# Seven block products for the last two tiles of the first layer, second-layer weights begun during the later attention pairs, k tail on 128 rows

## The chip, the cores and the metric

The kernel runs on one core of one Trainium2 chip. The metric is the device time of one execution in microseconds: before the change the median of three runs is 967.34 us (967.02 to 968.44).

## The reference, cut to what matters

Three parts, one behind the other, all in float32 (the weights of the two layers arrive as float64):

```python
def phi(x):                                   # attention features, 64 -> 2 x 128
    proj = x @ w_phi
    proj = proj - max(abs(proj), axis=-1)
    return concat([exp(proj), exp(-proj)])
num = phi(q) @ (phi(k).T @ v)                 # for 4 batches x 8 heads, 576 positions, 64 wide
den = phi(q) @ sum(phi(k)) + 1e-06
x = reshape(num / den)                        # 2304 x 512
h = x @ w_in;   x = maximum(0.01 * h, h) @ w_out      # first layer, 512 -> 2048 -> 512
h = x @ w_in2;  out = (h * sigmoid(h)) @ w_out2       # second layer, 512 -> 2048 -> 512
```

## The kernel before, in words

**Number format.** TensorE multiplies in the fast rounded form of float32. To keep the precision every operand is split into a rounded high part and the rest (`split`, L428: ScalarE copies into the rounded form, VectorE subtracts through `sub`, L125), and each product is three matmuls: high by high, high by low, low by high.

**Attention.** Heads are taken in 16 pairs. Pairs 0 to 7 are "full" pairs: plain float32 matmuls, which the machine does in two passes. Pairs 8 to 15 are "split" pairs with the three-matmul form; their denominators take a round trip through DRAM (`num_split`, L323: `e<-d`, `rec<-e`, `d<-rec`). The last 64 positions of k, the k tail, are done by `s_pkt` (L190): for a full pair by a matmul with 64 contraction rows (`kt[0:64]` by `wraw[0:64]`). The array `kt` already holds the tail twice, in rows 0 to 63 and 64 to 127; `BDF[:, 0]` is w_phi in rows 0 to 63 and zeros in rows 64 to 127. GpSimd finds the largest magnitude of each column over the partitions (`partition_all_reduce`, L227).

**Layer 1.** The 2304 rows of x are five tiles (`tiles1`, L86): two of 462 and three of 460 columns, as x is held transposed. For each tile t there are 16 chunks c of 128 of the 2048 hidden features. A step (t, c) is `emit_h` (L526: 12 matmuls, the leaky ReLU on ScalarE, the split into `gh` and `gl`) and, one step later, `emit_y` (L542: 12 matmuls into the four `y` banks of PSUM, which all 16 chunks of a tile fill). So a tile has 192 matmuls of each kind. In tile 0 the output weights are converted from float64 and saved in `wos`; later tiles load them again (`load_wo`, L488).

**Weights of layer 2.** Layer 2 works by seven block products in place of eight (the list `PRODUCTS`, L522). Its weights are made in 16 jobs (`prep_w7`, L446): two float64 loads with conversions (`load64`, `narrow64`), four sums, four splits and stores to `w7s`. `run_jobs` (L741) spends a credit per step; a job costs 1.8 + 1.8 + 1.8 + 1.6 = 7.0 credits. Before the change it starts when the last attention step has been issued, with 3.4 credits a step. The loads use three rotating buffers (`raw`).

**Order.** The program order of attention against layer 1 comes from due times: attention steps have offsets (`OFF0`, `OFF1`), layer-1 steps have a time `T0 + pace(s + 1)` for s = 16 t + c (L712 to L716), and `run_att` issues what is due. From that program a planner makes each engine's fixed queue when the kernel is built: it plays the program through with assumed durations and lets each engine take the ready instruction that stands first in the program. So work far down in the program can be placed early if its inputs and buffers are there. On the chip each queue is strictly in order. All loads and stores but two go through one queue, SP's. The first twelve weight loads are held back by tokens: GpSimd copies one number, which exists only after a given pair's `partition_all_reduce`, into the buffer that the load then overwrites (`PACE`, L68; L406 to L409).

## Time and profile before

| | before |
|---|---|
| median of the runs | 967.34 us |
| profiled execution | 967.73 us, span 965.9 us, mean granted clock 0.998 |
| TensorE (PE) busy | 947.5 us, 98% of the span |
| weight loads (PEld) busy | 886.1 us, 92% |
| VectorE (DVE) busy | 648.7 us, 67% |
| ScalarE (ACT) busy | 597.1 us, 62% |
| GpSimd (POOL) busy | 78.4 us, 8% |
| HBM read, written | 177.82 MB, 47.22 MB |

Busy times are a union over an engine's instructions. Matmuls overlap in the array, so the duration of one (some 370 ns in layer 1) is not its cost; its cost is the distance to the next one's start. The shares are averages over the span, and the stages differ, so the rows below are by stretch.

Attention's full pairs run from the start to about 110 us; the first matmul of layer 1 starts at 113.7 us, and the split pairs run between layer 1's matmuls until about 410 us. Layer 1 alone, with the weight jobs, runs to 613 us, layer 2 from there to the end (its first products start earlier, between the last steps of layer 1).

### The profile page before, as it was taken

The numbers are of one execution on the slowest core, as the hardware profiler recorded it, in microseconds if no ns is written. First come the engines' busy times: TensorE is split into PE (matmuls) and PEld (weight loads), VectorE is DVE, ScalarE is ACT, GpSimd is POOL, SyncE is SP. The second block draws the span as 40 slices with busy tenths as digits, with TensorE's granted clock in tenths as the row PEclk, the third lists the DMA queues.
The fourth block names the chain that finished last, engine by engine and source line by source line (L and its number), as shares of the span: only waits on it lengthen the run. The fifth ranks groups of instructions, "written<-read, shape, count | busy, mean of one in ns | idle before, by whom it ended". The sixth has DMA issues, their size and how long they took to land.

```text
span 965.9 us, 15759 instructions
## 1 busy us (share of the span) xinstructions
PE 947.5 (98%) x5376; PEld 886.1 (92%) x5376; DVE 648.7 (67%) x1279; ACT 597.1 (62%) x1224; POOL 78.4 (8%) x56
## 2 busy tenths in 40 slices
PE   7999999989999999999999999999999999999998
PEld 6888888979899999988888999999999999999998
DVE  6677799985666665278777767778762585624853
ACT  6567687867777777466656556556554565544553
POOL 3334300121111101000000000000000000000000
PEclk9999999999999999999999999999999999999999
DMA  6333477873344232299999999896989778997884
GB/s 218 100 108 102 154 242 252 304 245 118 96 118 119 93 106 93 90 321 367 377 345 318 373 356 353 281 371 233 320 285 297 239 234 271 291 294 216 249 278 138
DMA packets 102384, 226.13 MB, mean 234 GB/s; under 512 B 15008, under 2 KB 24992, under 8 KB 102304
## 3 DMA queue, kind: packets, MB, share of 16 engines
q1 hardware_dynamic: 102016, 224.86, 69.5%
q8 instruction: 43, 0.70, 0.3%
q14 instruction: 37, 0.30, 0.1%
q10 hardware_dynamic: 288, 0.26, 0.1%
HBM read 177.82 MB, written 47.22 MB: 233 GB/s over the span
## 4 chain that ended last, share of the span: by engine, by line
PE 80%; DMA 8%; DVE 6%; ACT 4%; issue 1%; SPq 1%; DVEq 0%; ACTq 0%
PE ps_y L688 18%; PE ps_y L552 17%; PE ps_a L533 16%; PE ps_a L612 10%; PE ps_y L612 8%; PE ps_a L268 2%; PE ps_a L302 2%; DMA d<-rec 2%; PE ps_a L334 2%; DMA rec<-e 1%; PE ps_y L268 1%; DMA e<-d 1%; DMA raw<-in_moe_w_in_dram 1%; PE ps_a L180 1%; DMA w7s<-wst 1%
## 5 line engine op out<-in xcount | busy, mean ns | idle before, releaser
L552 PE MATMUL ps_y<-gh,wo 128*128 128x460 f32 (+1 forms) x640 | 198.6, 374 | 1.9 <-ACT gh L429 1.9
L688 PE MATMUL ps_y<-gt,ws 128*128 128x384 f32 x1008 | 177.2, 336 | 0.0
L688 PEld LDWEIGHTS ps_y<-gt,ws 128*128 128x128 f32 x1008 | 176.5, 188 | 0.0
L552 PEld LDWEIGHTS ps_y<-gh,wo 128*128 128x128 f32 x640 | 120.5, 189 | 16.2 <-ACT gh L429 3.1
L552 PE MATMUL ps_y<-gl,wo 128*128 128x460 f32 (+1 forms) x320 | 118.3, 374 | 3.0 <-DVE gl L126 3.0
L533 PE MATMUL ps_a<-xh,wih 128*128 128x460 f32 (+1 forms) x320 | 119.5, 373 | 0.3 <-ACT g L536 0.3
L533 PE MATMUL ps_a<-xl,wih 128*128 128x460 f32 (+1 forms) x320 | 118.8, 371 | 0.0
L533 PE MATMUL ps_a<-xh,wil 128*128 128x460 f32 (+1 forms) x320 | 118.7, 371 | 0.0
L612 PE MATMUL ps_a<-xs,ws 128*128 128x384 f32 x546 | 105.0, 338 | 0.5 <-DMA ws<-w7s 0.5
L612 PEld LDWEIGHTS ps_a<-xs,ws 128*128 128x128 f32 x546 | 96.8, 188 | 1.3 <-ACT g L604 0.8
L227 POOL PARTITION_ALL_REDUCE m<-p x32 | 72.8, 2279 | 297.3 <-ACT p L223 199.5
L429 ACT ACTIVATE gt<-g 128x384 fp32r<-128x384 f32 x120 | 62.8, 524 | 51.9 <-PE ps_y L688 49.8
L126 DVE TENSOR_TENSOR gt<-g,gt 128x384 fp32r<-128x384 f32 x120 | 66.5, 556 | 33.1 <-ACT gt L429 32.6
L612 PE MATMUL ps_y<-xs,ws 128*128 128x384 f32 x462 | 88.3, 338 | 0.2 <-DVE g L588 0.2
L612 PEld LDWEIGHTS ps_y<-xs,ws 128*128 128x128 f32 x462 | 81.7, 188 | 0.6 <-DVE g L588 0.5
L126 DVE TENSOR_TENSOR gl<-g,gh 128x460 fp32r<-128x460 f32 (+1 forms) x80 | 51.7, 647 | 33.4 <-ACT gh L429 30.4
L552 PEld LDWEIGHTS ps_y<-gl,wo 128*128 128x128 f32 x320 | 60.6, 190 | 10.6 <-DVE gl L126 3.9
L533 PEld LDWEIGHTS ps_a<-xh,wil 128*128 128x128 f32 x320 | 60.1, 188 | 6.8
L533 PEld LDWEIGHTS ps_a<-xh,wih 128*128 128x128 f32 x320 | 60.2, 188 | 6.7 <-ACT g L536 0.5
L533 PEld LDWEIGHTS ps_a<-xl,wih 128*128 128x128 f32 x320 | 60.2, 188 | 5.9
L536 ACT ACTIVATE g<-ps_a 128x460 f32<-128x460 f32 (+1 forms) x80 | 44.0, 552 | 34.6 <-PE ps_a L533 32.8
L420 ACT ACTIVATE t<-raw 128x512 f32<-128x512 f32 x64 | 42.6, 668 | 15.1 <-DVE wst L126 6.5
(142 smaller groups left out, 1560.2 us busy)
## 6 DMA issues: line engine op xcount, KB each, us to landing
ws<-w7s SPq DMA_DIRECT2D x336, 256.0 KB, 3.8
wo<-wos SPq DMA_DIRECT2D x64, 512.0 KB, 5.4
w7s<-wst SPq DMA_DIRECT2D x48, 512.0 KB, 5.9
raw<-in_moe_w_in_dram SPq DMA_DIRECT2D x32, 512.0 KB, 5.0
raw<-in_moe_w_out_dram SPq DMA_DIRECT2D x32, 512.0 KB, 5.8
wos<-wo SPq DMA_DIRECT2D x16, 512.0 KB, 3.1
va<-in_v_dram SPq DMA_DIRECT2D x16, 325.0 KB, 3.6
qr<-in_q_dram SPq DMA_DIRECT2D x16, 288.0 KB, 3.8
```

The lines of the kernel that those rows point to most:

```text
L126: nc.vector.tensor_tensor(out_, x, h.bitcast(F32), op=ALU.subtract)
L227: nc.gpsimd.partition_all_reduce(m, p, 128, bass_isa.ReduceOp.absmax)
L268: nc.tensor.matmul(pv[:, s, j], ke[:, 2 * c + j, s, :], vf[:, w : w + NKV], start=False, stop=(j == 1 and c == 3), skip_group_check=True)
L302: nc.tensor.matmul(pb[:, w : w + NNUM], e[:, s, cs], KV[:, s, j], start=(s == 0), stop=(s == 1))
L334: nc.tensor.matmul(o, lhs, st[m, a][:, s, j * w : (j + 1) * w], start=(n == 0), stop=(n == 5))
L420: nc.scalar.activation(t, hi.bitcast(F32), AF.Abs)
L429: nc.scalar.activation(h, f, AF.Copy)
L533: nc.tensor.matmul(ph, a[:, kk, :], b_[:, kk, :], start=(m == 0), stop=(m == 3 * KD - 1))
L536: nc.scalar.activation(g, ph, AF.Prelu, alpha=0.01)
L552: nc.tensor.matmul(Y[t][d][:, 0:n], a[:, ds_], b_, start=(c == 0 and m == 0), stop=(c == NC - 1 and m == 2))
L612: nc.tensor.matmul(bank[b_], w[:, a, kk], x[:, c, kk], start=(first and m == 0), stop=(m == 5), skip_group_check=True)
L688: nc.tensor.matmul(bank[b_][db], w[:, a, db], t[:, c], start=(first and p == 0 and m == 0), stop=(p == NP - 1 and m == 2), skip_group_chec ...
```

## The change

Four edits, in one diff:

1. Tiles 3 and 4 (`TA`, `TB`) are taken together for x W_in: two tiles by two chunks make a 2 x 2 block product over two halves of the 512 contraction rows, done by the seven products of `PRODUCTS`, each of six matmuls (`h1_ops`). The sums of x are made once (`prep_x1`), those of the weights for every pair of chunks (`combine`). Results of tile TA are split and used at once; those of TB are kept in float32 in `G4` (in buffers of the weights no longer needed) and split later (`split_g4`), and TB's output products come last, on their own.
2. The layer-2 weight jobs begin at step s = 17 with 2.0 credits a step while attention is still running; then 3.4 a step, 4.0 a pair of chunks, 1.0 a chunk of TB. Loads issued while attention is unfinished wait for a token of the last `partition_all_reduce` that was issued. In that stage the stores' buffers are taken from `raw` too.
3. The k tail of a full pair is a matmul on all 128 rows.
4. Buffers are moved between pools (`attc`, `w2`, `s0`), so that the new tiles fit.

```diff
-    WH = const.tile([128, F], F32R, name="WH")
+    WH = attc.tile([128, F], F32R, name="WH")
...
-            nc.tensor.matmul(o, st["kt"][0:64], wraw[0:64], start=True, stop=True)
+            nc.tensor.matmul(o, st["kt"], BDF[:, 0], start=True, stop=True)
...
-            if a == 1 and full(i):
+            if not full(i):
+                last[0] = 2 * i + a
+                nc.gpsimd.tensor_copy(token[:, last[0] : last[0] + 1], m[0:1, 0:1])
+            elif a == 1:
...
-        if nconv[0] < len(PACE) and PACE[nconv[0]] is not None:
-
+        if nconv[0] < len(PACE):
             g = PACE[nconv[0]]
+        else:
+            g = last[0] if nconv[0] >= 2 * NC and seq else None
+        if g is not None:
             nc.gpsimd.tensor_copy(raw.bitcast(F32)[0:1, 0, 0:1], token[:, g : g + 1])
...
-            o = wp.tile([128, m, 2, 256], F32R, tag="wo1", bufs=WOB, name="wst")
+            if w2p[0] is None:
+                o = wp.tile([128, m, 2, 256], F32R, tag="raw", bufs=RAWB, name="wst")
+            else:
+                o = wp.tile([128, m, 2, 256], F32R, tag="wo1", bufs=WOB, name="wst")
...
+    def prep_x1():
+
+        for i in (2, 3, 4, 5):
+            TX[i] = s0p[0].tile([128, 2, 2, N1], F32R, tag="tx", bufs=4, name="tx")
+        for kk in range(2):
+            b = []
+            for k_ in (kk, kk + 2):
+                b1 = wp.tile([128, 2, N1], F32, tag="raw", bufs=RAWB, name="b1")
+                for j, t in enumerate((TA, TB)):
+                    xh, xl = X1[t]
+                    nc.vector.tensor_tensor(b1[:, j], xh[:, k_].bitcast(F32), xl[:, k_].bitcast(F32), op=ALU.add)
+                b.append(b1)
+            b1, b2 = b
...
+            nc.vector.tensor_tensor(t1, b1[:, 1], b1[:, 0], op=ALU.subtract)
+            nc.vector.tensor_tensor(t2, b2[:, 1], t1, op=ALU.subtract)
+            nc.vector.tensor_tensor(t3, b2[:, 1], b1[:, 1], op=ALU.subtract)
+            nc.vector.tensor_tensor(t4, b2[:, 0], t2, op=ALU.subtract)
+            for i, x in ((4, t2), (5, t3), (3, t1), (2, t4)):
+                split(x, TX[i][:, 0, kk], TX[i][:, 1, kk])
+
+    def combine(p):
+
+        f = []
+        for c in (2 * p, 2 * p + 1):
+            x = s0p[0].tile([128, 512], F32, tag=f"f{c % 2}", name="f")
+            h, l = (w.rearrange("p k f -> p (k f)").bitcast(F32) for w in wi[0, c])
+            nc.vector.tensor_tensor(x, h, l, op=ALU.add)
+            f.append(x)
+        fa, fb = f
+        lo, hi = slice(0, 256), slice(256, 512)
+        nc.vector.tensor_tensor(fb[:, hi], fb[:, lo], fb[:, hi], op=ALU.add)
+        nc.vector.tensor_tensor(fb[:, lo], fa[:, lo], fb[:, lo], op=ALU.subtract)
+        nc.vector.tensor_tensor(fa[:, lo], fb[:, hi], fa[:, lo], op=ALU.subtract)
+        nc.vector.tensor_tensor(fa[:, hi], fa[:, hi], fa[:, lo], op=ALU.subtract)
+        for x, ids in ((fa, (4, 6)), (fb, (5, 3))):
+            o = s0p[0].tile([128, 2, 2, 2, 128], F32R, tag="cw", bufs=4, name="cw")
+            split(x, o[:, 0].rearrange("p m k f -> p (m k f)"), o[:, 1].rearrange("p m k f -> p (m k f)"))
...
+    def h1_ops(p):
+
+        bank = [ps("a")[:, 0:N1], ps("a")[:, 0:N1]]
...
+        for n, (b_, wi_, xi, first) in enumerate(PRODUCTS):
+            m = 0
+            for kk in range(2):
+                for a, c in ((0, 0), (0, 1), (1, 0)):
+                    nc.tensor.matmul(bank[b_], w1_of(p, wi_, a, kk), x1_of(xi, c, kk), start=(first and m == 0), stop=(m == 5), skip_group_check=True)
+                    m += 1
+            if n == 0:
+                v1 = hold(bank[0])
+            elif n == 1:
+                leaky(2 * p, 0, bank[1], v1)
+            elif n == 2:
+                u2 = hold(bank[0])
+            elif n == 3:
+                v7 = hold(bank[1])
+            elif n == 4:
+                leaky(2 * p + 1, 1, bank[0], v7)
+            elif n == 5:
+                leaky(2 * p + 1, 0, bank[1], u2)
+            else:
+                leaky(2 * p, 1, bank[0])
+            yield
...
-    RATE = (3.4, 9.0)
+    RATE = (2.0, 3.4, 4.0, 1.0, 9.0)
...
+    def close_att():
+        att_ctx.close()
+        w2p[0] = ctx.enter_context(tc.tile_pool(name="w2", bufs=1))
+        s0p[0] = s0_ctx.enter_context(tc.tile_pool(name="s0", bufs=1))
+        settle()
+        prep_x1()
+        combine(0)
+
+    for s, (t, c) in enumerate((t, c) for t in range(TA) for c in range(NC)):
...
-        if not seq and s1p[0] is None:
-            att_ctx.close()
-            s1p[0] = ctx.enter_context(tc.tile_pool(name="s1", bufs=1))
-        if s1p[0] is not None:
-            run_jobs(RATE[0])
...
+        if s > NC:
+            run_jobs(RATE[w2p[0] is not None])
+        if not seq and w2p[0] is None:
+            close_att()
...
+    ys = y_groups(*prev)
+    for p in range(NC // 2):
+        for c in (2 * p, 2 * p + 1):
+            wo[c] = load_wo(c)
+        if p + 1 < NC // 2:
+            combine(p + 1)
+        for _ in h1_ops(p):
+            next(ys, None)
+        for _ in ys:
+            pass
+        ys = (y for c in (2 * p, 2 * p + 1) for y in y_groups(TA, c))
+        run_jobs(RATE[2])
...
+    for c in range(NC):
+        if c + 3 < NC:
+            wo[c + 3] = load_wo(c + 3)
+            split_g4(c + 3)
+        emit_y(TB, c)
+        run_jobs(RATE[3])
+        if c in (1, 4):
+            settle()
+            next(x_first)
+        if c >= 9:
+            next(h_first)
```

In `h1_ops`, `hold(x)` is a ScalarE copy out of the bank, and `leaky(c, j, x, v)` adds the held value on VectorE (where there is one), applies the leaky ReLU on ScalarE and, for TA (j = 0), splits. `y_groups` is `emit_y` given out in groups of three matmuls, one for each of the four `y` banks.

## Rows read from the trace of the kernel before

**Rows 1.** The page: engine PE's busy time; shares of the chain that ended last.

```profile
PE 947.5 (98%) x5376; PEld 886.1 (92%) x5376; DVE 648.7 (67%) x1279; ACT 597.1 (62%) x1224; POOL 78.4 (8%) x56
...
PE 80%; DMA 8%; DVE 6%; ACT 4%; issue 1%; SPq 1%; DVEq 0%; ACTq 0%
```

**Rows 2.** Windows: stretch, length; busy us (instructions) per engine; clock, DMA share, GB/s.

```profile
125.00:200.00 75.00, 71.69 (x362) 63.84 (x360) 71.32 (x136) 58.56 (x109) 5.24 (x2) 1.00 0.79 268
200.00:225.00 25.00, 25.00 (x147) 23.33 (x148) 19.30 (x38) 19.00 (x41) 3.28 (x2) 0.93 0.66 218
225.00:400.00 175.00, 174.09 (x1062) 162.14 (x1061) 99.92 (x197) 123.63 (x270) 27.19 (x13) 1.00 0.35 102
400.00:425.00 25.00, 23.41 (x112) 20.35 (x111) 12.79 (x27) 11.61 (x24) 0.00 (x0) 1.00 0.67 227
425.00:550.00 125.00, 125.00 (x600) 112.40 (x599) 98.04 (x193) 75.41 (x140) 0.00 (x0) 1.00 0.98 353
...
615.00:950.00 335.00, 334.35 (x1902) 333.46 (x1901) 207.84 (x403) 182.24 (x381) 0.00 (x0) 1.00 0.85 276
```

**Rows 3.** Timeline of PE around one k tail: start, duration, instruction, count.

```profile
32.83 0.61 PE L302 MATMUL ps_a<-KV,qh 128*128 128x96 f32 x4
33.37 0.48 PE L195 MATMUL ps_a<-wc,kt 64*128 64x128 f32 x2
33.79 0.70 PE L180 MATMUL ps_a<-wc,kr 128*128 128x256 f32 x2
```

**Rows 4.** Timeline of PE, 195 to 208 us (idle before it, releaser, in brackets).

```profile
195.89 1.10 PE L552 MATMUL ps_y<-gh,wo 128*128 128x462 f32 x4 [0.33 <-ACT gh L429]
199.97 0.47 PE L552 MATMUL ps_y<-gl,wo 128*128 128x462 f32 x1 [2.98 <-DVE gl L126]
...
206.05 1.93 PE L268 MATMUL ps_a<-va,ke 128*128 128x112 f32 x16
207.82 0.40 PE L262 MATMUL ps_a<-va,ke 128*128 128x130 f32 x2
```

**Rows 5.** Timeline of DVE in the same stretch.

```profile
197.05 1.52 DVE L422 TENSOR_SCALAR t<-t 128x512 f32<-128x512 f32 x1
...
199.29 0.63 DVE L126 TENSOR_TENSOR gl<-g,gh 128x462 fp32r<-128x462 f32 x1
```

**Rows 6.** Timeline of POOL in the same stretch.

```profile
196.62 2.69 POOL L227 PARTITION_ALL_REDUCE m<-p  x1 [13.42 <-DVE ql L126]
```

**Rows 7.** Timeline of SP's queue: loads of layer-2 weights before 225 us.

```profile
183.73 0.33 SPq L411 DMA_DIRECT2D raw<-in_moe_w_in_dram  x1
...
207.93 0.49 SPq L411 DMA_DIRECT2D raw<-in_moe_w_in_dram  x1
```

**Rows 8.** Groups by line, whole span: count; busy us, mean ns; idle before, releasers.

```profile
L126 DVE TENSOR_TENSOR gl<-g,gh 128x460 fp32r<-128x460 f32 (+1 forms) x80 | 51.7, 647 | 33.4 <-ACT gh L429 30.4 <-PE ps_y L552 2.6
L429 ACT ACTIVATE gh<-g 128x460 fp32r<-128x460 f32 (+1 forms) x80 | 46.8, 584 | 6.8 <-PE ps_y L552 5.6
L424 DVE SCALAR_TENSOR_TENSOR t<-raw,t 128x512 uint32<-128x512 uint32 x64 | 45.8, 718 | 0.9
...
L420 ACT ACTIVATE t<-raw 128x512 f32<-128x512 f32 x64 | 42.6, 668 | 15.1 <-DVE wst L126 6.5 <-DVE r L425 3.7 <-DMA raw<-in_moe_w_in_dram 2.6
...
L422 DVE TENSOR_SCALAR t<-t 128x512 f32<-128x512 f32 x64 | 29.5, 462 | 13.2 <-ACT t L420 12.2
...
L126 DVE TENSOR_TENSOR wst<-s,wst 128x512 fp32r<-128x512 f32 x32 | 22.0, 689 | 10.9 <-ACT wst L429 10.8
...
L588 DVE TENSOR_TENSOR g<-ps_a,hs 128x384 f32<-128x384 f32 x39 | 21.7, 557 | 29.2 <-PE ps_a L612 29.0
...
L356 DVE TENSOR_TENSOR x<-x,d 128x288 f32<-128x288 f32 x16 | 7.3, 459 | 33.1 <-DMA d<-rec 33.1
...
L466 DVE TENSOR_TENSOR s<-r,s 128x256 f32<-128x256 f32 x16 | 6.8, 423 | 0.4
```

**Rows 9.** DMA issues in 425 to 550 us: count, KB each, median us to landing.

```profile
wo<-wos SPq DMA_DIRECT2D x25, 512.0 KB, 6.2
```

More of the change, by code (lines that the diff above doesn't have):

```diff
@@ L104, in tile_linear_attention_ffn_ffn @@
     P = [dict() for _ in range(B * HP)]
-    token = const.tile([1, NFULL], F32, name="token")
+    token = const.tile([1, 2 * B * HP], F32, name="token")
+    last = [None]
     nconv = [0]
@@ L547, in emit_y, with group @@
             Y[t] = [ps("y") for _ in range(KD)]
-        for d in range(KD):
+        def group(d):
             ds_ = slice(d * 128, (d + 1) * 128)
+            y = Y[t][d][:, 0:n]
             for m in range(3):
                 a, b_ = ((oh, gh), (oh, gl), (ol, gh))[m]
-                nc.tensor.matmul(Y[t][d][:, 0:n], a[:, ds_], b_, start=(c == 0 and m == 0), stop=(c == NC - 1 and m == 2))
-        if c == NC - 1:
-            for d, y in enumerate(Y.pop(t)):
+                nc.tensor.matmul(y, a[:, ds_], b_, start=(c == 0 and m == 0), stop=(c == NC - 1 and m == 2))
+            if c == NC - 1:
@@ L555, in emit_y @@
                 o = gp.tile([128, n], F32, tag="o", name="o", bufs=3)
                 if d % 2 == 0:
-                    nc.vector.tensor_copy(o, y[:, 0:n])
+                    nc.vector.tensor_copy(o, y)
                 else:
-                    nc.scalar.activation(o, y[:, 0:n], AF.Copy)
+                    nc.scalar.activation(o, y, AF.Copy)
                 nc.sync.dma_start(x2[d, :, tiles1[t][0] : tiles1[t][0] + n], o)
+        for d in range(KD):
+            yield group(d)
+    def emit_y(t, c):
+        for _ in y_groups(t, c):
+            pass
@@ new lines, in tile_linear_attention_ffn_ffn @@
+    TA, TB = len(tiles1) - 2, len(tiles1) - 1
+    N1 = tiles1[TA][1]
+    TX, CW = {}, {}
+    def prep_x1():
[10 more added lines that the diff above has]
+            b1, b2 = b
+            t1, t3 = (wp.tile([128, N1], F32, tag="t64", bufs=2, name="t1") for _ in range(2))
+            t2, t4 = (wp.tile([128, N1], F32, tag="r64", bufs=2, name="t2") for _ in range(2))
+            nc.vector.tensor_tensor(t1, b1[:, 1], b1[:, 0], op=ALU.subtract)
[4 more added lines that the diff above has]
+                split(x, TX[i][:, 0, kk], TX[i][:, 1, kk])
@@ new lines, in w1_of, with x1_of, hold, leaky @@
+    def w1_of(p, i, a, kk):
+        if i < 3:
+            return wi[0, 2 * p + (i == 2)][a][:, kk + 2 * (i > 0), :]
+        return CW[p, i][:, a, kk]
+    def x1_of(i, a, kk):
+        if i in TX:
+            return TX[i][:, a, kk]
+        return X1[TB if i == 6 else TA][a][:, kk + 2 * (i > 0), :]
+    def h1_ops(p):
+        bank = [ps("a")[:, 0:N1], ps("a")[:, 0:N1]]
+        def hold(x):
+            v = gp.tile([128, N1], F32, tag="o", name="o", bufs=3)
+            nc.scalar.activation(v, x, AF.Copy)
+            return v
+        def leaky(c, j, x, v=None):
+            if j:
+                g = wp.tile([128, N1], F32, tag="wil", bufs=NC, name="g4")
+            else:
+                g = gp.tile([128, N1], F32, tag="g", name="g", bufs=2)
+            if v is not None:
+                nc.vector.tensor_tensor(g, x, v, op=ALU.add)
+                x = g
+            nc.scalar.activation(g, x, AF.Prelu, alpha=0.01)
+            if j:
+                G4[c] = g
+                return
+            gh = gp.tile([128, N1], F32R, tag="gh", name="gh", bufs=2)
+            gl = gp.tile([128, N1], F32R, tag="gl", name="gl", bufs=2)
+            split(g, gh, gl)
+            G[TA, c] = (gh, gl)
+        for n, (b_, wi_, xi, first) in enumerate(PRODUCTS):
[16 more added lines that the diff above has]
+                leaky(2 * p + 1, 0, bank[1], u2)
+            else:
+                leaky(2 * p, 1, bank[0])
+            yield
@@ L562, in tile_linear_attention_ffn_ffn, with split_g4 @@
+    G4 = {}
+    def split_g4(c):
+        tags = ("g", "g") if c % 3 == 2 else ("gh", "gl")
+        gh, gl = (gp.tile([128, N1], F32R, tag=tag, name="gh", bufs=2) for tag in tags)
+        split(G4.pop(c), gh, gl)
+        G[TB, c] = (gh, gl)
     WS = {}
@@ L657, in operand @@
             else:
[L658 removed]
+                t = w2p[0].tile([128, 2, NB], F32R, tag="wo2", bufs=4, name="gt")
             tl.append(t)
@@ L757, in tile_linear_attention_ffn_ffn @@
         prev = (t, c)
-        if not seq and s1p[0] is None:
-            att_ctx.close()
-            s1p[0] = ctx.enter_context(tc.tile_pool(name="s1", bufs=1))
-        if s1p[0] is not None:
-            run_jobs(RATE[0])
-            if t == len(tiles1) - 1:
-                if c in (2, 5):
-                    settle()
-                    next(x_first)
-                if c >= 9:
-                    next(h_first)
-    emit_y(*prev)
+        if s > NC:
+            run_jobs(RATE[w2p[0] is not None])
+        if not seq and w2p[0] is None:
+            close_att()
+    run_att(1e9)
+    if w2p[0] is None:
+        close_att()
+    ys = y_groups(*prev)
[7 more added lines that the diff above has]
+        for _ in ys:
+            pass
+        ys = (y for c in (2 * p, 2 * p + 1) for y in y_groups(TA, c))
+        run_jobs(RATE[2])
+    s0_ctx.close()
+    s1p[0] = ctx.enter_context(tc.tile_pool(name="s1", bufs=1))
+    for c in range(3):
+        wo[c] = load_wo(c)
+        split_g4(c)
+    for _ in ys:
+        pass
+    for c in range(NC):
[9 more added lines that the diff above has]
+            next(h_first)
     nothing = iter(())
```

20 lines of the change are left out of this document (11 added, 9 removed).

## Prediction

> **What bounds the kernel now.** I read the page first: PE is busy for 947.5 of 965.9 us, and the chain that ended last lies on PE for 80% of the span [rows 1]. An average over stages can hide a stage with another limit, so next come the windows [rows 2]. The reader is to see two things. PE has no idle time that matters from 225 to 400 us (174.09 of 175), from 425 to 550 us (125.00 of 125) and in layer 2 (334.35 of 335). It loses time in two places: 3.3 us in 125 to 200 us, with the granted clock at 0.93 just behind it, and 1.6 us in 400 to 425 us, where attention ends. And the other engines are not free: DVE is at 95% in 125 to 200 us (71.32 of 75), at 57% in 225 to 400, at 78% in 425 to 550; ACT at 71% in 225 to 400 and 60% in 425 to 550. So a matmul taken away is worth its full distance to the next one, as long as DVE and ACT keep up with PE; the question of this case is whether they do once the work added to them is in.
>
> **The change part by part.** The sum is made against the profiled execution, 967.73 us (span 965.9), which is 0.39 above the median of the runs, 967.34.
>
> *Products.* Tiles 3 and 4 had 2 x 16 x 12 = 384 matmuls with W_in; now 8 pairs of chunks x 7 products x 6 = 336. That is 48 fewer of 460 columns. 425 to 550 us holds only such work, 600 matmuls in 125.00 us: 0.208 us each [rows 2]. 48 x 0.208 = **-10.0 us**. The output products stay at 192 a tile.
>
> *k tail.* In a full pair the last L302 matmuls are followed by two passes with 64 rows, then by L180 [rows 3]. Sixteen float32 passes on 128 rows, 112 columns wide, take 207.82 - 206.05 = 1.77 us, 0.111 each [rows 4]. Four L302 take 0.54 us to the next start: three of 0.111, and 0.21 for the last, which has the 64-row pass behind it. The two tail passes take 0.42 to the start of L180. So 0.63 us now; with three starts 0.111 apart, 0.33. That is 0.3 us a pair, 2.4 for eight, if PE is the limit there. The trace has no 128-row tail: the bounds are -2.4 and 0 (PE only waits elsewhere). I take **-2.0**, nearer to the row, as one of eight may be hidden. [...]
>
> *Weight jobs, moved.* Five layer-2 loads were placed early by the planner, at 183.73 to 207.93 us [rows 7], and their conversions fell into the stretch where DVE is at 95%. A conversion costs DVE two operations like L422 and two like L424 (2 x 0.462 + 2 x 0.718 = 2.36 us) and ACT two like L420 (1.34) [rows 8]; five cost 11.8 and 6.7 us. In that stretch PE waits 2.98 us for `gl` [rows 4], which stands on DVE behind such work and comes at 199.29 [rows 5]; the clock dip after it costs 0.07 x 25 = 1.75 us [rows 2]. Now these loads can't be issued before s = 17, and they wait for a token. What is late next there is the last of W_out's own conversions, which stay. Bounds: -4.7 (all gone) and 0; I take **-3.0**.
>
> The jobs' new place: steps 17 to 40 (the last due attention step, 128.4, falls below T0 + pace(s + 1) first at s = 40) with 2.0 credits make 48, about seven jobs of 7.0. A job costs DVE two conversions, four sums like L466 and splits of three and a half times 0.689: 4.72 + 1.69 + 2.41 = 8.8 us; ACT four like L420 and three and a half copies like L429: 2.67 + 2.04 = 4.7 us [rows 8]. Seven jobs are 62 and 33 us. With them 225 to 400 us has DVE at 99.9 + 62 = 162 of 175 us (92%) and ACT at 123.6 + 33 = 157 (90%), in queues in strict order, where DVE already stands still for 33.1 us in all at L356, waiting for the denominators' DMAs [rows 8]. Every job also issues two loads and four stores on SP's queue, 2.8 MB, so those small DMAs wait longer. A load waits for its token on GpSimd, and behind it in that queue stands the next `partition_all_reduce`; POOL is busy for 27 of 175 us, so that has room. The nearest rows for the price in PE time are these: at DVE 78%, ACT 60% PE lost nothing in 125 us (0); at DVE 95%, ACT 78% it lost 3.3 and 1.75 us in 100 us, which over 175 us is 8.8. I take **+2.5**: PE's own work there is 98% dense, but at a lower DVE load than in the bad stretch.
>
> *End of attention.* `prep_x1` and `combine(0)` stand in the program ahead of all later steps: 24 DVE operations like `gl` (15.5 us) and 2 x 0.69 + 4 x 0.42 + 2 x 0.69 = 4.4 us, a burst of 20 us on DVE; ACT 4.7 + 1.2. All of it needs the last pair's x, so it can't be placed earlier. Behind it waits the `gl` of the following steps. PE can meanwhile do a few h blocks (12 x 0.208 = 2.5 us each, four `a` banks) and the y blocks whose `gl` is done: some 12 to 15 us. Bounds 0 and +6 (with the wait at 400 to 425 us standing as it is).
>
> *The paired tiles.* A pair of chunks is 42 + 24 = 66 matmuls, 13.7 us on PE. DVE gets `combine` 4.4, three adds like L588, wider, 0.65 each (estimate: 0.557 x 460/384), two `gl` (1.3) and 4.0/7 of a job (5.0): 12.7 us, 93%. From the burst to the end of TB DVE has some 187 us of work (nine jobs 79, `combine` 35.5, burst without it 15.5, adds 15.6, `gl` 25, x of layer 2 and the rest 16) for 185 us on PE (7 x 5.0 + 110 + 40). It fits only because jobs slip: in the window 425 to 550 us they ran behind their place in the program without PE waiting. The last jobs, of W_out2, are not needed until the output products of layer 2, where DVE is at 62%. Bounds: 0, and 5% of 150 us as in the stretch at 95%, +8. For these two parts together I take **+4.0**.
>
> *TB's output products.* A chunk is 12 x 0.208 = 2.5 us, and 512 KB of `wo` have to land in each; with loads three chunks ahead there are 7.5 us for one, against 6.2 at a DMA share of 0.98 [rows 9]. 0, as jobs are nearly out by then. The y banks change owner with no h block between, but four groups apart. If it fails, see the third rival.
>
> Pools moved, tokens copied: nothing, as POOL is free.
>
> Sum: -10.0 - 2.0 - 3.0 + 2.5 + 4.0 = -8.5, from 967.7 to 959.2; for the median 0.4 less, **958.8 us**. Its own range, with the bounds not all at one end: 953 to 965.
>
> **The rivals.**
>
> *All of the new work is hidden.* For it: in 425 to 550 us DVE at 78% cost PE nothing, and the planner can order around a burst. Against: DVE goes to over 90% for 360 us. Time: 967.3 - 10.0 - 2.4 - 4.7 = 950.2.
>
> *DVE takes PE's place, slower than before.* Place: from s = 17 to the end of TB, 175 + 185 = 360 us. Price: the lost share of the one stretch at DVE 95%, 5.05 us in 100 [rows 2], over 360 us: +18.2. Against it stand -10.0 - 2.0 - 3.0. Time: 967.3 - 15.0 + 18.2 = 970.5; a little more, 974, if ACT at 90% adds to it. It decides once PE waits for over 15 us in all. For it: 187 us of DVE work for 185 us; jobs stand ahead of `h1_ops` in program order, so PE's needs come second. Against: jobs are held back by three buffers and DMAs of 6 us, which leaves DVE gaps for the others. A collision adds to it: an L422 beside the all-reduce of 196.62 took 1.52 us [rows 5, 6] against 0.462 in the mean; 13 all-reduces in 225 to 400 us could lengthen DVE's work by 13 x 1.06 = 14 us, to 100% there. [...]
>
> *It does not do what it says: products go, time does not.* TB without h blocks has nothing to cover a late `wo`: with landings of 10 us (6.2 doubles nearly when jobs and layer 2's first loads fall into the same 40 us) a buffer comes round every 12.5 us for four chunks, 3.1 us a chunk instead of 2.5, +8 in 13 chunks; with 4.0 + 2.5 from above the sum is about 967. Against: the jobs' earlier start takes DMAs out of this time.
>
> **How the numbers follow.** Forecast 0.47, all hidden 0.20, DVE-bound 0.21, TB's loads 0.12. Faster by over 0.2% (below 965.4; 0.2% is about what a measurement of this kernel can tell): forecast, all hidden and a tenth of the last, 0.68. Within 0.2%: most of the last, 0.10. Slower: 0.22. The range goes from 949 to 974, into both sides.
>
> **What would show it.** Right: L533 down to 576 matmuls beside 336 of the new line; three starts 0.11 apart at the tail; no 3 us wait near 197 us and no dip; PE idle of no more than a few us in 225 to 400 and behind the end of attention, layer 1 ending about 8 us sooner and layer 2 unchanged. Wrong: PE waits for `gl` or a bank behind DVE, in sum over 12 us; gaps ended by `wo` in TB; DVE over 95% from the end of attention on, with the clock dipping.

## The result, and the profile after

The change makes the kernel slower: the median of four runs is 977.32 us (974.32 to 982.16), against 967.89 us for the kernel before (four runs, 967.02 to 969.47). The ratio is 1.0101, 95% interval 1.0079 to 1.0124. The forecast of 958.8 us had the wrong sign, and the time lies above its range (949 to 974). The profiled execution took 979.34 us (span 977.2), 11.3 us more span than before.

The page after, engines and the shares of the chain that ended last, against [rows 1]:

```profile
PE 942.7 (96%) x5328; PEld 876.4 (90%) x5328; DVE 697.9 (71%) x1391; ACT 618.6 (63%) x1272; POOL 90.2 (9%) x84
...
PE 65%; DMA 12%; DVE 11%; ACT 9%; issue 2%; SPq 1%; POOL 0%; DVEq 0%; ACTq 0%
```

The 48 matmuls are gone, yet PE lies on only 65% of the chain (80% before), and DMA, DVE and ACT have taken the rest. The windows say where (same columns as [rows 2]):

```profile
125.00:200.00 75.00, 72.48 (x361) 64.36 (x360) 71.37 (x136) 58.50 (x107) 7.35 (x4) 0.99 0.74 252
200.00:225.00 25.00, 24.60 (x148) 22.66 (x148) 14.53 (x27) 18.51 (x40) 5.49 (x6) 0.96 0.56 167
225.00:400.00 175.00, 162.89 (x972) 147.10 (x971) 128.04 (x253) 134.02 (x287) 33.77 (x32) 1.00 0.53 168
400.00:425.00 25.00, 23.64 (x118) 20.56 (x118) 16.82 (x37) 13.24 (x30) 1.00 (x2) 1.00 0.48 168
225.00:440.00 215.00, 198.69 (x1147) 178.38 (x1146) 156.50 (x315) 153.59 (x330) 34.77 (x34) 1.00 0.53 170
440.00:550.00 110.00, 109.13 (x515) 97.40 (x514) 101.07 (x209) 72.86 (x141) 0.00 (x0) 0.98 0.88 298
...
628.00:965.00 337.00, 336.85 (x1919) 336.36 (x1918) 202.13 (x393) 181.56 (x379) 0.00 (x0) 1.00 0.83 268
```

From 225 to 400 us PE was idle for 0.9 us before [rows 2] and is for 12.1 now. The reader is to compare two lines here. From 225 to 440 us DVE is at 73% and ACT at 71%, and PE loses 16.3 us. From 440 to 550 us DVE is at 92%, and PE loses 0.9. A busy share does not tell which stretch is the tight one; the first has attention with the denominators' round trip in it, the second hasn't.

Four marks cut the 11.3 us into stages (us from the span's start, read from PE's timeline): where the output products of step 16 begin (the first step of tile 1), where attention's last matmul ends (the start of the next one), where the output products of step 47 begin (the last step before the paired tiles), and where layer 1's output products end:

| | before | after | stage, forecast | stage, measured |
|---|---|---|---|---|
| step 16 begins | 215.9 | 213.3 | -5.0 | -2.6 |
| attention ends | 397.4 | 414.5 | +2.5 | +19.7 |
| step 47 begins | 447.7 | 467.9 | with the next | +3.1 |
| layer 1 ends | 616.6 | 628.0 | -6.0 | -8.8 |

Layer 2 takes as long as before; it carries the 11.3 us to the end.

The tail, PE's timeline of after, against [rows 3]:

```profile
32.32 1.17 PE L307 MATMUL ps_a<-KV,qh 128*128 128x96 f32 x9
33.33 0.41 PE L197 MATMUL ps_a<-wc,kt 128*128 128x128 f32 x2
33.58 0.60 PE L182 MATMUL ps_a<-wc,kr 128*128 128x256 f32 x2
```

Nine passes take 1.01 us to the first of the tail, 0.112 each, with no longer last one, and the two tail passes 0.25 to the next start instead of 0.42.

Now the pair stage. First DVE, then ACT, then PE of after, in the part where PE first loses time:

```profile
227.07 0.75 DVE L244 TENSOR_TENSOR m<-p,m 128x576 f32<-128x576 f32 x1
231.88 0.46 DVE L361 TENSOR_TENSOR x<-x,d 128x288 f32<-128x288 f32 x1 [4.06 <-DMA d<-rec]
232.26 0.75 DVE L128 TENSOR_TENSOR ql<-e,qh 128x576 fp32r<-128x576 f32 x1
...
235.30 0.43 DVE L429 TENSOR_SCALAR t<-t 128x512 f32<-128x512 f32 x1 [1.11 <-ACT t L427]
...
237.22 1.21 DVE L429 TENSOR_SCALAR t<-t 128x512 f32<-128x512 f32 x1 [0.23 <-ACT t L427]
...
239.37 0.27 DVE L128 TENSOR_TENSOR KVL<-ps_a,KVH 128x128 fp32r<-128x128 f32 x1
239.56 0.68 DVE L431 SCALAR_TENSOR_TENSOR t<-raw,t 128x512 uint32<-128x512 uint32 x1
240.16 0.68 DVE L128 TENSOR_TENSOR wst<-r,wst 128x512 fp32r<-128x512 f32 x1
240.76 0.68 DVE L432 CUSTOM_DVE_ANT_0 r<-t,r 128x1024 uint16<-128x1024 uint16 x1
241.37 0.63 DVE L128 TENSOR_TENSOR gl<-g,gh 128x462 fp32r<-128x462 f32 x1
```

```profile
228.57 0.68 ACT L256 ACTIVATE qh<-e 128x576 fp32r<-128x576 f32 x1
...
232.37 0.45 ACT L292 ACTIVATE xh<-x 128x288 fp32r<-128x288 f32 x1 [2.55 <-DVE x L361]
232.72 0.67 ACT L256 ACTIVATE qh<-m 128x576 fp32r<-128x576 f32 x1
234.61 0.66 ACT L427 ACTIVATE t<-raw 128x512 f32<-128x512 f32 x1 [1.21 <-DMA raw<-in_moe_w_in_dram]
```

```profile
238.42 0.40 PE L339 MATMUL ps_a<-qh,KVH 128*128 128x288 f32 x1 [0.36 <-ACT g L546]
239.69 0.40 PE L339 MATMUL ps_a<-qh,KVL 128*128 128x288 f32 x1 [0.75 <-DVE KVL L128]
242.05 0.48 PE L565 MATMUL ps_y<-gl,wo 128*128 128x462 f32 x1 [0.65 <-DVE gl L128]
244.72 0.40 PE L339 MATMUL ps_a<-qh,KVL 128*128 128x288 f32 x1 [0.26 <-DVE KVL L128]
246.25 0.40 PE L221 MATMUL ps_a<-qs,WH 128*128 128x288 f32 x1 [0.47 <-DVE ke L159]
247.44 0.48 PE L543 MATMUL ps_a<-xh,wih 128*128 128x462 f32 x1 [0.65 <-ACT x L343]
```

DVE stands for 4.06 us at L361, which waits for the denominators. ACT's next instruction, the split of that x, waits for L361 and stands too. DVE's queue keeps its order meanwhile: its next operation, the `ql` at 232.26 us, has had its `qh` from ACT since 229.25 us (228.57 + 0.68), and still runs only behind L361. Then comes a job: ACT waits 1.21 us for its load, DVE 1.11 us for ACT, and from 235.30 on DVE works with hardly a gap (0.23 us at 237.22), a job's operations (L429 to L432, `wst`) and what PE needs (`KVL`, `gl`) in turn. PE ran from its stock until then (one wait of 0.40 us since 205 us), and now waits for each of the latter. No single wait is long, and no single releaser stands out.

From the list of waits of 205 to 440 us (engine and line waited for: us in total, times, longest us), first before, then after:

```profile
DVE x L356 <- DMA d<-rec: 33.1, 16, 4.9
...
ACT xh L287 <- DVE x L356: 30.2, 14, 4.2
```

```profile
DVE x L361 <- DMA d<-rec: 23.2, 14, 4.1
ACT xh L292 <- DVE x L361: 19.2, 11, 3.5
...
DVE t L429 <- ACT t L427: 12.1, 9, 4.6
...
ACT t L427 <- DMA raw<-in_moe_w_in_dram: 10.7, 6, 3.5
...
PEld ps_y L565 <- DVE gl L128: 6.4, 6, 2.1
```

The wait for the denominators was there before, and longer, while PE lost 2.5 us in all in the same 235 us. The chain of waits of after from 222 to 440 us goes through it all the same:

```profile
by line: DMA d<-rec 13.6%; DMA rec<-e 13.3%; DMA e<-d 9.3%; issue 5.9%; DMA raw<-in_moe_w_in_dram 4.2%; ACT d L342 3.3%; DVE m L244 3.2%; ACT x L343 3.0%; SPq L352 2.5%; DVE wst L128 2.3%; DVE x L361 2.2%; DMA wo<-wos 2.1%; ACT ke L168 1.9%
```

The three transfers of the round trip make 36% of it, and of the thirteen lines named none is PE's. In the kernel before they make 19% of the same stretch, behind PE's own lines with 20% and 19%:

```profile
by line: PE ps_y L552 20.4%; PE ps_a L533 18.9%; DMA d<-rec 8.3%; PE ps_a L268 8.1%; PE ps_a L334 6.6%; DMA rec<-e 5.6%; DMA e<-d 4.8%; DMA w7s<-wst 3.5%; issue 1.9%; SPq L347 1.3%; DVE x L356 1.3%; PE ps_a L219 1.3%; PE ps_a L220 1.2%; PE 
```

### The profile page after: what moved, and what is told of

It is laid out like the page before. It is cut to its first block, busy times and chain, and to the rows that moved or that the text cites. A ratio compares the mean times of both kernels' runs of the same rounds, so it can differ in the third digit from the quotient of the medians.

```text
span 977.2 us, 15859 instructions
## 1 busy us (share of the span) xinstructions
PE 942.7 (96%) x5328; PEld 876.4 (90%) x5328; DVE 697.9 (71%) x1391; ACT 618.6 (63%) x1272; POOL 90.2 (9%) x84
## 4 chain that ended last, share of the span: by engine, by line
PE 65%; DMA 12%; DVE 11%; ACT 9%; issue 2%; SPq 1%; POOL 0%; DVEq 0%; ACTq 0%
PE ps_y L820 18%; PE ps_y L565 13%; PE ps_a L744 10%; PE ps_y L744 8%; PE ps_a L667 7%; PE ps_a L543 4%; DMA d<-rec 3%; DMA rec<-e 3%; DMA e<-d 2%; DMA raw<-in_moe_w_in_dram 2%; PE ps_a L307 2%; PE ps_y L273 1%; DVE m L244 1%; DVE r L432 1%; ACT d L342 1%
## 5 line engine op out<-in xcount | busy, mean ns | idle before, releaser
L565 PEld LDWEIGHTS ps_y<-gh,wo 128*128 128x128 f32 x704 | 132.9, 190 | 20.0 <-issue 3.6
L565 PE MATMUL ps_y<-gl,wo 128*128 128x462 f32 (+1 forms) x256 | 95.8, 380 | 6.7 <-DVE gl L128 6.4
L543 PE MATMUL ps_a<-xh,wih 128*128 128x462 f32 (+1 forms) x192 | 72.7, 379 | 4.5 <-DVE ke L159 1.8
L543 PE MATMUL ps_a<-xl,wih 128*128 128x462 f32 (+1 forms) x192 | 71.4, 372 | 0.0
L543 PE MATMUL ps_a<-xh,wil 128*128 128x462 f32 (+1 forms) x192 | 71.2, 371 | 0.0
L436 ACT ACTIVATE gh<-g 128x460 fp32r<-128x460 f32 (+1 forms) x80 | 46.4, 584 | 12.1 <-PE ps_y L565 10.9
L128 DVE TENSOR_TENSOR gl<-g,gh 128x462 fp32r<-128x462 f32 (+1 forms) x64 | 41.3, 647 | 13.2 <-ACT gh L436 12.6
L428 ACT ACTIVATE r<-raw 128x512 uint32<-128x512 uint32 x64 | 42.4, 668 | 8.5 <-DVE wst L128 5.2
L736 ACT ACTIVATE g<-g 128x384 f32<-128x384 f32 x72 | 37.1, 520 | 16.7 <-DVE g L720 16.5
L432 DVE CUSTOM_DVE_ANT_0 r<-t,r 128x1024 uint16<-128x1024 uint16 x64 | 45.9, 719 | 1.4
```

The source lines that it names most:

```text
L128: nc.vector.tensor_tensor(out_, x, h.bitcast(F32), op=ALU.subtract)
L428: nc.scalar.activation(r, lo, AF.Copy, scale=2.0**-29)
L432: nc.vector.tensor_tensor(r, tu, r, op=ALU.add)
L436: nc.scalar.activation(h, f, AF.Copy)
L543: nc.tensor.matmul(ph, a[:, kk, :], b_[:, kk, :], start=(m == 0), stop=(m == 3 * KD - 1))
L565: nc.tensor.matmul(y, a[:, ds_], b_, start=(c == 0 and m == 0), stop=(c == NC - 1 and m == 2))
```

## The experiments

The theory at this point: the jobs' place is the whole loss, and it is lost not to a full engine but to queues in strict order, which stand at the denominators' round trip; the jobs take the slack that hid it. The rivals: DVE has no room (the forecast's second rival), the jobs' DMAs delay the small ones, and the end of attention with the paired tiles is too dense.

**Is it the moved jobs?** One kernel leaves them until attention is over, one has them alone, one takes their token away.

```diff
-    RATE = (2.0, 3.4, 4.0, 1.0, 9.0)          # e1, from after
+    RATE = (0.0, 3.4, 4.0, 1.0, 9.0)
...
+        if s > NC and s1p[0] is None:          # e2, from before; with the tokens of after
+            run_jobs(2.0)
...
-            g = last[0] if nconv[0] >= 2 * NC and seq else None      # e3, from after
+            g = None
```

> The changed kernel with RATE[0] = 0: no weight job is issued before attention ends; all 16 then follow at the later rates. If the moved jobs are the whole loss (they cost some 20 us between 205 and 440 us), PE is dense there again (attention's last output matmul near 397 us, as before, less 2) and the time falls from 977 to 955-962, unless the backlog of 16 jobs now makes DVE the limit in the paired tiles: then PE shows waits for DVE between 460 and 620 us and the time is 962-972. If the loss has another cause (the pools moved, the planner's order as a whole), the stretch 205 to 440 us stays 20 us too long and the time stays above 970.

> The kernel before plus only the moved jobs (2.0 credits a step from s = 17, tokens, stores from the raw buffers). If the move alone makes the loss: 985-992, PE waits of some 20 us between 205 and 440 us. If the loss needs the products or the tail edit beside it: 965-970.

> The changed kernel without the token in the moved loads, so that they are issued as soon as a buffer is free and land before they are needed. If ACT's waits for late loads and GpSimd's waits for raw buffers (which hold back the next all-reduce) make the loss: 955-965. If it is the conversions' own place in ACT's and DVE's queues: 972-982, the waits for raw gone and PE's waits still there. As the loads are no longer spread, it may also get worse, above 982, with the DVE-bound stretch before 205 us back.

| us | median | ratio to before | end of attention | step 47 | end of layer 1 |
|---|---|---|---|---|---|
| before | 966.73 | | 397.4 | 447.7 | 616.6 |
| e1, jobs late | 1005.26 | 1.0383 [1.0345, 1.042] | 399.3 | 447.4 | 619.0 |
| e2, move alone | 984.78 | 1.0193 [1.0151, 1.0235] | 413.7 | 464.5 | 633.4 |
| e3, no token | 989.05 | 1.0232 [1.0195, 1.0268] | 422.8 | 472.0 | 636.4 |

Without jobs the pair stage is nearly as dense as before (PE loses 3.9 us in 205 to 440 us, 2.5 before), and step 47 comes at 447.4, with the burst of sums for the paired tiles issued ahead of it. From attention's end to step 47 it takes 48.1 us, against 50.3 before. So that burst costs nothing, and the jobs in attention are nearly the whole loss up to there: step 16 to step 47 takes 22.8 us longer in after than before, and 2.6 longer in e1. Alone, in the kernel before, the jobs put step 47 16.8 us later. Without the tokens, and so without the spreading of the loads, it is worse. But e1 is by far the slowest of the three, and above both ranges expected for it if the jobs are the loss: the jobs left over cost 11.5 us in the paired tiles (step 47 to the end of layer 1 takes 171.6 us, 160.1 in after) and some 36 us in layer 2. PE's timeline of e1:

```profile
673.18 2.29 PE L820 MATMUL ps_y<-gt,ws 128*128 128x384 f32 x6 [2.14 <-DMA ws<-w7s]
695.61 2.29 PE L744 MATMUL ps_a<-xs,ws 128*128 128x384 f32 x6 [20.14 <-ACT xs L436]
701.88 0.69 PE L744 MATMUL ps_a<-xs,ws 128*128 128x384 f32 x1 [3.98 <-ACT xs L436]
```

And ACT's timeline of e1, where `xs` (x of layer 2) stands behind the jobs' operations in the queue:

```profile
693.32 0.65 ACT L428 ACTIVATE r<-raw 128x512 uint32<-128x512 uint32 x1
693.96 0.63 ACT L436 ACTIVATE wst<-s 128x512 fp32r<-128x512 f32 x1
694.49 0.65 ACT L427 ACTIVATE t<-raw 128x512 f32<-128x512 f32 x1
695.05 0.51 ACT L436 ACTIVATE xs<-b 128x384 fp32r<-128x384 f32 x1
```

**Is it the round trip?** The denominators' DMAs are left out of after (e5) and, as the control, of before (e8).

```diff
-        e = at([96, w // 48], F32, "e6")
-        for j in range(2):
-            nc.sync.dma_start(e[48 * j : 48 * j + 48], d[64 - 64 * j : 65 - 64 * j])
-        nc.vector.reciprocal(e, e)
-        nc.sync.dma_start(rec[i, a].rearrange("(p f) -> p f", p=96), e)
-        st["r", a] = d
-        for j in range(2):
-            nc.sync.dma_start(d[64 * j : 64 * j + 64], rec[...])
+        st["r", a] = x
```

> The changed kernel with the denominators' DMA round trip left out (x is multiplied by itself instead of by the reciprocal; the output is not the reference's). All of ACT's and DVE's other work stays, and the jobs too. If the queues lose their time standing at L361 for the round trip, with the jobs having taken the slack in which they used to recover: PE dense between 205 and 440 us, 955-962. If it is the work of the jobs as such in the queues: 970-980.

> Control: the kernel before with the denominators' DMA round trip left out in the same way (output not the reference's). Before the change DVE stood 33 us at this wait and PE lost almost nothing by it. If that slack is why it cost nothing: 963-967 (only the 2 us at the end of attention go). If the round trip cost PE time before as well, as much as the 13.5 us it costs in the changed kernel: 953-957, and then it is no explanation of the loss.

| | with round trip | without |
|---|---|---|
| before: median | 967.89 us | 964.21 us |
| before: step 16, step 47, between them | 215.9, 447.7, 231.8 | 219.4, 447.4, 228.0 |
| after: median | 977.32 us | 963.79 us |
| after: step 16, step 47, between them | 213.3, 467.9, 254.6 | 212.9, 453.3, 240.3 |
| the change costs: median, between steps 16 and 47 | +9.4 us, +22.8 | -0.4 us, +12.3 |

Ratios to before: e5 0.996 [0.9946, 0.9975], e8 0.997 [0.9952, 0.9989]. The round trip cost the kernel before some 3 us (967.49 beside e8, less 964.21), and costs the changed one 13.5. The marks have to be read as distances here. The profiled execution of e8 took 967.44 us, 3.2 more than e8's median, and came late to layer 1 (its first matmul at 117.50 us, 113.70 before, with a granted clock of 0.88 in the first 25 us, against 1.00 before), in a part that the edit leaves alone; taken by step 47 alone the round trip would get 14.3 of 20.2 us. From step 16 to step 47, 10.5 of the 22.8 us exist only with the round trip, which fits the medians (9.4 + 0.4 = 9.8). The other 12.3 are lost without it as well. The windows of 225 to 440 us (columns as above), e5 and then e8, speak against a lack of DVE's time as the cause of the part that went:

```profile
225.00:440.00 215.00, 207.27 (x1210) 189.81 (x1209) 172.47 (x334) 164.03 (x347) 33.34 (x34) 1.00 0.53 180
```

```profile
225.00:440.00 215.00, 214.86 (x1266) 199.74 (x1265) 124.30 (x233) 149.55 (x318) 27.91 (x13) 1.00 0.39 125
```

In e5 DVE is busier than in after (80% against 73%), ACT too (76% against 71%), and PE loses 7.7 us instead of 16.3. But it is not dense, as the expectation had it, and the time lies between the two ranges given there: in e8, without the moved jobs, PE loses 0.1 us. What e5 doesn't part: with the DMAs some reciprocals and SP's issues have gone as well.

**How many jobs?** Half the rate in attention (e4), a third with faster spending later (e10), none with faster spending later (e9, e9b).

```diff
-    RATE = (2.0, 3.4, 4.0, 1.0, 9.0)
+    RATE = (1.0, 3.4, 4.0, 1.0, 9.0)          # e4
+    RATE = (0.6, 3.4, 5.0, 2.0, 9.0)          # e10
+    RATE = (0.0, 3.4, 5.5, 2.0, 9.0)          # e9
+    RATE = (0.0, 4.5, 6.5, 2.5, 9.0)          # e9b
```

> The changed kernel with 1.0 instead of 2.0 credits a step while attention runs. If the loss in 205 to 440 us grows with the work put there: about half of it left (10-12 us, attention's last output matmul near 406 us against 397 with none and 414 with 2.0). If a single wait or the token makes it, the loss stays near 20 us. The total also holds what the later stages lose when more jobs are left for them (the version with none lost 30 us in layer 2), so it can lie anywhere in 968-992.

> 0.6 credits a step beside attention (two jobs of 16), then 3.4, 5.0, 2.0. If the loss grows with the work put beside attention (none: 0, half: 8, full: 20 us by the 48th step of layer 1): 3-5 us lost there, layer 2's loss gone: 956-964.

> The version with no jobs beside attention, the rates after it raised from 4.0 to 5.5 a pair of chunks and from 1.0 to 2.0 a chunk of TB, so that some 14.5 of the 16 jobs are issued before layer 2 instead of 10. If the 30 us that the version without them lost in layer 2 were W_out2's weights being late and nothing else: 953-962, both kernels beaten. If DVE can't take seven products' sums and the jobs in the same stretch: waits for DVE in 460 to 620 us, 965-985.

> As the one before, with 4.5, 6.5 and 2.5 credits: all 16 jobs issued before layer 2 (4.5 x 7 + 52 + 40 = 123). In program order DVE would have 7.7 + 8.2 = 15.9 us of work for each 13.7 us of a pair of chunks. If jobs ahead in program order delay PE's own needs: PE waits in 460 to 580 us, 965-980; if they slip behind as they did before the change: 953-960.

| us | median | ratio | end of attention | step 47 | jobs in attention (24 steps x rate / 7.0) |
|---|---|---|---|---|---|
| e1 | 1005.26 | 1.0383 | 399.3 | 447.4 | 0 |
| e9 | 984.69 | 1.0169 [1.0147, 1.019] | 396.2 | 444.3 | 0 |
| e9b | 991.78 | 1.0239 [1.0214, 1.0263] | 399.4 | 447.5 | 0 |
| e10 | 976.31 | 1.0087 [1.0066, 1.0108] | 401.7 | 449.8 | 2.1 |
| e4 | 980.34 | 1.0129 [1.0109, 1.0148] | 407.5 | 455.4 | 3.4 |
| after | 977.32 | 1.0101 [1.0079, 1.0124] | 414.5 | 467.9 | 6.9 |

The dose decides the time of step 47: 2.4 us for 2.1 jobs, 8.0 for 3.4, 20.5 for 6.9. Counted from step 16, which the runs don't reach at the same time, it is 5.2, 8.1 and 20.2 us, that is 2.5, 2.4 and 2.9 a job; that each job costs more than the one before is not shown. (e1, e9 and e9b do the same until attention ends; they differ by 3.2 us at step 47, by 1.4 counted from step 16.) What is saved there is lost later: PE loses 5.9 us in 650 to 700 us in e10, 10.5 in e9, 25.2 in e1, none in after. No rate beats the kernel before, and e9b and e10 came out slower than any range expected for them. One in between (e10) is at best level with after.

**Which part of a job?** From e1 on, in the same steps as after: the DMAs of jobs alone, with tokens (e7); their ACT and DVE work on data that is there already, unpaced (e6) and behind the same tokens (e12); of the latter, DVE's half (e13) and ACT's half (e14). All are extra work: the real jobs still follow after attention, so only the marks up to step 47 are compared, and each is one run.

```diff
-        if s > NC:
-            run_jobs(RATE[w2p[0] is not None])
+        if s > NC and w2p[0] is not None:
+            run_jobs(RATE[1])
+        if s > NC and w2p[0] is None:
+            run_extra(2.0)                     # loads and stores of a job, or its conversions, sums and splits
```

> The same base plus the DMAs of the moved jobs alone: loads behind tokens into the raw buffers, stores of the same bytes from there, no conversion. If the DMA traffic lengthens the round trip and that makes the loss: 10-20 us between 205 and 440 us. If it is the work in the queues: under 5 us, last output matmul of attention at 397-402.

> The version with no jobs beside attention (its 30 us of loss in layer 2 stay), plus the ACT and DVE work of the moved jobs alone, on data that lie in SBUF already (2.0 credits a step, no load, no store, no token; results unused). If the conversions' place in the strict queues makes the loss: PE loses 12-20 us between 205 and 440 us, attention's last output matmul at 408-414 us. If DMA traffic or late loads make it: under 5 us, 397-402.

> The version with no jobs beside attention plus the moved jobs' ACT and DVE work, each conversion held back by a token as the real ones are; no load, no store, results unused. If the work in the queues is the loss: attention's last output matmul at 408-414 us (399 with none, 414.5 in the changed kernel), the 48th step's output matmuls at 458-468 (447 and 468). If the early burst made the loss of the unpaced version: 400-404 and 448-452.

> The same with the DVE operations alone (8.8 us a job; no ACT operation). If DVE's queue carries the loss, as most of the standing at the round trip is DVE's: nearly all of e12's loss, last output matmul at 406-413. If it is ACT's or the chain between the two: under a third, 399-403.

> The same with the ACT operations alone (4.7 us a job). If ACT's queue carries it, being the busier one beside attention (71% against 57%): 406-413. If DVE's: under a third of e12's loss, 399-403.

| us | one run | end of attention | step 47 | later than e1 there |
|---|---|---|---|---|
| e7, DMAs | 1000.51 | 402.7 | 450.5 | +3.1 |
| e6, work, unpaced | 1030.99 | 425.1 | 473.2 | +25.8 |
| e12, work, paced | 1010.27 | 410.1 | 457.9 | +10.5 |
| e13, DVE's half | 1004.24 | 407.4 | 455.3 | +7.9 |
| e14, ACT's half | 1006.1 | 408.8 | 457.8 | +10.4 |
| after, whole jobs | 977.32 | 414.5 | 467.9 | +20.5 |

e6 missed its purpose: without a load to wait for, the work came in bursts, which e12 mends. The DMAs alone cost 3.1 us, no more than e1, e9 and e9b differ among themselves. DVE's half alone costs three quarters of what both halves cost together, ACT's half all of it, which neither a full DVE nor a full ACT explains. (Counted from step 16: e7 2.8, e12 11.9, e13 8.2, e14 11.6, after 20.2.) The windows of 205 to 440 us (columns as above), first e13, then e14:

```profile
205.00:440.00 235.00, 227.45 (x1312) 207.07 (x1311) 181.05 (x376) 154.45 (x332) 41.14 (x42) 0.99 0.36 111
```

```profile
205.00:440.00 235.00, 225.63 (x1309) 206.44 (x1308) 137.47 (x271) 176.63 (x381) 37.08 (x42) 0.99 0.36 112
```

In e14 DVE is busy for 58% and PE loses 9.4 us; in e13 ACT is at 66%, and PE loses 7.6 (in e1, without them, 3.9). A theory that names one queue alone falls. The program offers a reason, which these runs don't test by itself: nearly every result that PE needs passes through both engines (`gh` on ACT, then `gl` on DVE; `KVH`, then `KVL`; `qh`, then `ql`), so work on either delays the other. The three versions also share the tokens and the buffers that the extra work takes; of the tokens at least, little is seen: in 205 to 440 us no engine waits for GpSimd in e12 and e13, and in e14 ACT and DVE do for 2.7 us.

e12 and e7 add up to 13.6 of the 20.5 us (14.6 of 20.2 counted from step 16). The other 7 (5.6) belong to neither alone; what e12 lacks and after has is the load in front of the work (ACT waits 10.7 us for `raw` in after, and DVE 12.1 us for that ACT operation) and the `wo` wait told below. That these are the 7 us was not shown.

**Is the late side a lack of DVE time?** From e9, the six sums of `combine` go to GpSimd.

```diff
-            nc.vector.tensor_tensor(x, h, l, op=ALU.add)
+            nc.gpsimd.tensor_tensor(x, h, l, op=ALU.add)       # and the four that follow
```

> The version with no jobs beside attention at 5.5 and 2.0 credits after it (984.7 us), its weights' sums (six operations for each of the eight pairs of chunks, 24 us) done by GpSimd, which is idle there. If DVE's time is the limit after attention: the 31 us lost between 450 and 700 us fall by 10 to 24, 960-975. If it is the jobs' chain of buffers and DMAs, or GpSimd is slower than what it takes over and holds up the products: no change or worse, 980-1000.

991.5 us, 1.0249 [1.0232, 1.0266], worse than e9's 1.0169. Groups by line in 400 to 560 us (count; busy us, mean ns; idle before), first e9, then e15:

```profile
L128 DVE TENSOR_TENSOR gl<-g,gh 128x460 fp32r<-128x460 f32 x24 | 15.1, 634 | 0.8 <-ACT gh L436 0.8
L429 DVE TENSOR_SCALAR t<-t 128x512 f32<-128x512 f32 x18 | 7.6, 423 | 0.7 <-ACT t L427 0.3
```

```profile
L128 DVE TENSOR_TENSOR gl<-g,gh 128x460 fp32r<-128x460 f32 x23 | 18.8, 816 | 2.0 <-ACT gh L436 1.9
L429 DVE TENSOR_SCALAR t<-t 128x512 f32<-128x512 f32 x18 | 12.2, 682 | 3.7 <-ACT t L427 3.6
L613 POOL TENSOR_TENSOR f<-wih,wil 128x512 f32<-128x512 f32 x16 | 33.3, 2087 | 104.2 <-DVE cw L128 69.9 <-DVE xl L128 34.3
```

It settles nothing on the late side, as it took no load off DVE: operations beside GpSimd's became longer by 29% (`gl`) and 61% (L429). Whether late jobs are bound by DVE's time or by the chain of their buffers stays open.

**The tail alone**, on the kernel before:

```diff
-            nc.tensor.matmul(o, st["kt"][0:64], wraw[0:64], start=True, stop=True)
+            nc.tensor.matmul(o, st["kt"], BDF[:, 0], start=True, stop=True)
```

> The kernel before plus the k tail on 128 rows alone. By the distances of the passes 0.2-0.3 us a pair: layer 1's first matmul at 111.5-112 us instead of 113.7 and 965-966 in all, if the planner's order stays otherwise the same; 967 if later waits take it back.

965.15 us (964.03 to 967.94), 0.9976 [0.9962, 0.9989]; layer 1's first matmul starts at 112.48 us instead of 113.70. Of the kernels that compute the whole reference, this one alone beats the kernel before.

## Why the prediction was wrong

**Products, -10.0: right.** From step 47 to the end of layer 1 the time falls from 168.9 to 160.1 us, so -8.8, with L543 at 576 matmuls and L667 at 336. The missing 1 us is lost among the paired tiles.

**k tail, -2.0: right.** The marks of after give -1.85 at layer 1's first matmul, the tail alone -1.2 there and 2.3 us of time (0.24% of 967). The row decided rightly for a gain: passes on 128 rows follow at 0.112 to 0.125 us in after, the 64-row ones before at 0.21 ([rows 3], 0.42 for two).

**The wait near 197 us, -3.0: wrong, some -0.7.** The five early loads are gone, the wait is not; from layer 1's first matmul to step 16 it takes 101.5 us, against 102.2 before. PE's timeline of after, against the 2.98 us of [rows 4], then DVE's and GpSimd's:

```profile
197.38 0.48 PE L565 MATMUL ps_y<-gl,wo 128*128 128x462 f32 x1 [2.40 <-DVE gl L128]
```

```profile
195.79 1.53 DVE L128 TENSOR_TENSOR gl<-g,gh 128x462 fp32r<-128x462 f32 x1
```

```profile
195.24 2.43 POOL L229 PARTITION_ALL_REDUCE m<-p  x1 [11.57 <-DVE ql L128]
```

The clock dips as before: 0.97 in 175 to 200 us and 0.96 in 200 to 225 (1.00 and 0.93 before). DVE is as busy in 125 to 200 us as it was (71.37 us): the moved operations left a stretch that W_out's own conversions and attention fill anyway. The prediction saw that they would be late next, and still took 3.0 of the 4.7. What it did not see is that 0.9 of the 2.40 us is the `gl` itself, which took 1.53 us beside an all-reduce, against 0.62 for the next one.

**The jobs' new place, +2.5: the step that failed.** It measured +19.7 to the end of attention, outside its bounds (0 to +8.8). Two things were wrong in it. Its upper bound was the PE loss of another stretch, with DVE at 95% but no round trip in it, carried over by busy shares; the loss here arose at 73%. And the 33.1 us that DVE stood at L356 [rows 8] were named and then not priced. They were the slack and the danger in one: DVE and ACT stand together, 2 us in the mean and up to 4.9, and must catch up before PE's stock is used up. In the kernel before they mostly do; the control shows some 3 us for the whole trip. With jobs in both queues they don't, and 10.5 of the 22.8 us lost between steps 16 and 47 go when the trip goes. That is not quite half. The other 12.3 are lost without the trip too; e1, without jobs, loses 2.6, so most of them seem to come with the jobs, on either engine (e13, e14). By what wait these jobs' price without the trip arises stays open.

**End of attention and paired tiles, +4.0: about right in sum (4.3), by luck.** The burst that it priced costs nothing (e1), the paired tiles 1 us at DVE 92%. What is lost, 3.1 us from the end of attention to step 47, goes largely to a wait that the prediction did not see. PE's timeline of after:

```profile
439.41 0.45 PE L565 MATMUL ps_y<-gh,wo 128*128 128x460 f32 x1 [2.84 <-DMA wo<-wos]
```

These `wo` are only issued at 434.3 to 435.6 us, into buffers that open when attention's close (`load_wo`, L502), and the clock falls behind the gap (0.93 in 425 to 450 us).

**TB's loads, 0: right.** TB's output products run without a gap that is ended by `wo`.

**The rivals.** "DVE takes PE's place" (970.5, up to 974) came nearest in time and had the point right from which it decides: PE waits for more than 15 us, from the first jobs on. But it put the loss on DVE's time in all 360 us. DVE is not full in the first part, and where it is nearly full, behind step 47, PE loses next to nothing. Its collision of VectorE with GpSimd is there, but not at 14 us: in 225 to 440 us of after L429 takes 491 ns and L430 514, 12 of each, against 448 and 452 over the whole span, 1.3 us in all. Single ones count all the same: beside `gl` near 197 us there is the L429 at 237.22, 1.21 us long, right ahead of PE's first wait in the pair stage, with this all-reduce:

```profile
236.69 2.48 POOL L229 PARTITION_ALL_REDUCE m<-p  x1 [12.03 <-ACT p L225]
```

None of the three lasted until its all-reduce was over: the prediction's L422 [rows 5] ended at 198.57 us and its all-reduce [rows 6] at 199.31 (GpSimd's spans are rough), and the `gl` near 197 us and the L429 at 237.22 end before theirs, by 0.35 and 0.74 us. The token copies did no harm that shows: in 205 to 440 us of after nothing waits for GpSimd but SP's queue, for 1.7 us in three waits. "It does not do what it says" is refuted by layer 1's -8.8, "all hidden" by the pair stage.

**What stays open.** What makes up the 12.3 us that steps 16 to 47 lose without the round trip, and the 7 us (5.6 from step 16) between the parts and whole jobs, was not measured. The versions with parts of a job were run with the round trip only, once each.
